# Two decode layers over a key-value cache: heads loaded in pairs with 64-KB runs into three slots, 21 cache parts kept between the layers, weights by column halves, layer norm applied to products

## The chip, the cores and the metric

The kernel runs on one core of a Trainium2 chip. The metric is the device time of one execution in microseconds (us), lower is better. All tensors are float32 in HBM when it begins, and the result must be in HBM when it ends. One core has five engines with queues of their own: PE (TensorE, matrix products), DVE (VectorE), ACT (ScalarE), POOL (GpSimd) and SP (SyncE, which here only issues transfers), and 16 DMA engines that share out each transfer by partitions. The on-chip memory has 128 partitions; 4-byte elements are counted as floats per partition below.

## The reference, cut to what matters

Two tokens (batch 2, one position) of width 576 pass the same layer twice: attention over a given cache of 32 heads, 8192 keys each, head width 128, then a gated MLP of width 4608. Both passes use the same weights and the same cache.

```python
B, H, Sk, Dh, D, DF = 2, 32, 8192, 128, 576, 4608
def attention(x):                 # x: [2, 1, 576]
    q = (x @ wq).reshape(B, 1, H, Dh).transpose(0, 2, 1, 3)
    scores = einsum("bhqd,bhkd->bhqk", q, k_cache) * Dh ** -0.5
    o = einsum("bhqk,bhkd->bhqd", softmax(scores), v_cache)
    return o.transpose(0, 2, 1, 3).reshape(B, 1, H * Dh) @ wo
def mlp(x):
    return einsum("bsf,fd->bsd", gelu_tanh(x @ w_gate) * (x @ w_up), w_down)
for layer in range(2):
    x = x + attention(layernorm(x))
    x = x + mlp(layernorm(x))
```

K and V of one head and batch are 4 MiB each; 64 such heads make 512 MiB, read in each layer. wq and wo are 9.4 MB each, gate, up and down 10.6 MB each.

## The kernel before, in words

**Memory.** One tile `space` holds six slots of 4 MiB (32 KB a partition; a partition holds 64 consecutive keys of a head) and 1024 floats more. All loads come from it and all are issued by SP, in the order of one list: `queue` is filled when the program is built, `pump()` (L117) issues its head as soon as its place is free, and `done()` (L124) frees a place and pumps. So a load is issued right after the instruction that frees its place, and everything behind it in the list waits with it. Which slot a head gets is settled by `Arena.slot`, the one that came free first.

**Attention, per head and batch** (64 items a layer; `attention`, the loop over `n`). `query` (L392) spreads the query over 128 partitions by a product on PE. K comes in one transfer (L134) and is used in four parts of 16 keys a partition (1 MiB): DVE multiplies a part by the query in place (`multiply`, L409), POOL adds the upper half of the 128 products to the lower (L413), and DVE sums what is left (`add_up`, L418), which frees the part. `peak` (L432, L434) and `highest` (L438, L440) find the maximum over all keys by DVE, a transposition on PE, and DVE again, and spread it. `softmax` (L444, L447) is two activations, `total` (L453, L457) the sum and its reciprocal. `values` (L469) is 16 groups of four products of 512 columns on PE, with four groups of columns filling the array side by side; each four groups free a part of V. `gather` (L483, L485) on DVE, `context` (L494) on PE and `divide` (L499) bring both batches of a head into place. The order on each engine is written out by hand in the loop: item n's multiplies stand between item n-1's softmax steps.

**The joints.** In layer 0 the heads run forward, in layer 1 backward, so the last heads of layer 0 stay for layer 1: K of two items and V of three, 20 parts of 1 MiB. For K that stays, the products go to a place of their own (`products`), since the multiply otherwise overwrites K. Weights of layer 0's MLP, of wo and of layer 1's wq run through one slot and 1024 floats, a ring of four pieces of 2304 floats; layer 1's MLP uses the whole space. First loads of layer 1 are taken part by part, in an order written out.

**Weights.** wq, gate and up come in nine pieces each (`eighths`, L165): a row is cut into eight, and a partition reads four neighbouring ones, 8 KB for wq, 9216 bytes for gate and up. `project` (L511) uses wo in eight pieces, `lower` down (L620) in pieces of three rows a partition (6912 bytes), the last cut into two and one. Products with two rows of x fill 128 columns by groups of four.

**Layer norm.** `norm` (L338 to L361) works out mean and deviation, subtracts the mean from x, transposes the result on DVE (L354), and the factor 1/deviation is applied by ACT when the products are read (L379, L591, L592). The first product of a stage waits for it.

Of the kernel before, what the change touches and what calls it, by code (L numbers as in the profile page):

```python
# [24 lines left out]
J = SK // P  # L25
NHB = H * B
JC = 16

GH = 4
NU = 9  # L30
EQ = 512
EG = DF // 8
HG = EG // 2
NT = 4
NI = DF // (NT * P)
CW = D // 4

SLOT = J * DH
PART = JC * DH
NSLOT = 6  # L40
END = NSLOT * SLOT + 1024
RING = 5 * SLOT
HELD = 5


class Arena:


    def __init__(self):
        self.live = {}  # L50
        self.freed = [0] * (NSLOT + 1)
        self.clock = 0
        self.at = RING

    def clear(self, lo, n):
        return all(hi <= lo or l >= lo + n for l, hi in self.live.values())

    def slot(self, key, allowed):

        for s in sorted(allowed, key=lambda s: self.freed[s]):  # L60
            if self.clear(s * SLOT, SLOT):
                for k in range(4):
                    self.quarter(key, s * SLOT, k)
                return s * SLOT
        return None

    def quarter(self, key, at, k):
        lo = at + k * PART
        if not self.clear(lo, PART):
            return False  # L70
        self.live[key, k] = (lo, lo + PART)
        return True

    def ring(self, key, n, lo, hi=None):

        for at in [self.at, lo] + sorted(end for _, end in self.live.values()):
            if lo <= at and at + n <= (hi or END) and self.clear(at, n):
                self.live[key] = (at, at + n)
                self.at = at + n
                return at  # L80
        return None

    def free(self, key):
        lo, hi = self.live.pop(key)
        self.clock += 1
        for s in range(lo // SLOT, (hi - 1) // SLOT + 1):
            self.freed[s] = self.clock
# [3 lines left out]
def decode_layers(ctx, tc, x_in, kc, vc, wq, wo, wg, wu, wd, out):  # L91
# [9 lines left out]

    space = consts.tile([P, END], F32, name="space")

    x = consts.tile([P, CW], F32, name="x")
    nc.vector.memset(x, 0.0)
    for c in range(4):
        for s in range(2):
            lo = 32 * c + s * B
            nc.scalar.dma_start(
                x[lo:lo + B, :], x_in[:, :, c * CW:(c + 1) * CW].rearrange("b s d -> (b s) d")  # L110
            )


    arena = Arena()
    queue, ready, slots = [], {}, {}

    def pump():  # L117
        while queue:
            t = queue[0][1]()
            if t is None:  # L120
                return
            ready[queue.pop(0)[0]] = t

    def done(key):  # L124
        arena.free(key)
        pump()

    def cache(key, src, hb, allowed, pieces=1, where=None, part=None):

        rows = src[hb % B, hb // B].rearrange("(p j) d -> p j d", p=P)  # L130

        def load(at, lo, hi):
            t = space[:, at:at + SLOT].rearrange("p (j d) -> p j d", d=DH)
            nc.sync.dma_start(t[:, lo:hi, :], rows[:, lo:hi, :])  # L134
            return t

        def make():
            at = arena.slot(key, allowed)
            if at is None:
                return None  # L140
            slots[key] = at
            for lo in range(0, J, J // pieces):
                t = load(at, lo, lo + J // pieces)
            return t

        def make_quarter(k):
            at = slots[key] = RING if where == "ring" else slots[where]
            return load(at, k * JC, (k + 1) * JC) if arena.quarter(key, at, k) else None

        if where is None:  # L150
            queue.append((key, make))
        else:

            for k in [(NU + i) % 4 if where == "ring" else i for i in range(4)] if part is None else [part]:
                queue.append((key, lambda k=k: make_quarter(k)))

    def eighths(key, w, u, width, lo, hi=None):

        def make():
            at = arena.ring(key, 4 * width, lo, hi)  # L160
            if at is None:
                return None
            t = space[:, at:at + 4 * width].rearrange("p (c w) -> p c w", c=4)
            src = w.rearrange("r (e w) -> (r e) w", w=width).rearrange("(p j) w -> p j w", p=P)
            nc.sync.dma_start(t, src[:, 4 * u:4 * u + 4, :])  # L165
            return t

        queue.append((key, make))

    def down(key, t0, lo, hi, first):  # L170

        def make():
            at = arena.ring(key, (hi - lo) * D, first)
            if at is None:
                return None
            t = space[:, at:at + (hi - lo) * D].rearrange("p (i c) -> p i c", c=D)
            src = wd[t0 * P * NI:(t0 + 1) * P * NI, :].rearrange("(p i) c -> p i c", i=NI)
            nc.sync.dma_start(t, src[:, lo:hi, :])
            return t

        queue.append((key, make))

    def products():

        def make():
            ends = [END - k * PART for k in (2, 1, 0)]
            if not arena.clear(ends[0], 2 * PART):
                return None
            for k in range(2):
                arena.live["products", k] = (ends[k], ends[k + 1])  # L190
            return ends[:2]

        queue.append(("products", make))

    def out_rows(key, g, lo):

        def make():
            at = arena.ring(key, GH * D, lo)
            if at is None:
                return None  # L200
            t = space[:, at:at + GH * D].rearrange("p (i c) -> p i c", c=D)
            rows = GH * DH
            nc.sync.dma_start(t, wo[g * rows:(g + 1) * rows, :].rearrange("(p i) c -> p i c", i=GH))
            return t

        queue.append((key, make))

    DOWN = [(t, lo, lo + 3) for t in range(NT) for lo in (0, 3, 6)]
    DOWN[-1:] = [(NT - 1, 6, NI - 1), (NT - 1, NI - 1, NI)]
    every, front = range(NSLOT), range(HELD)  # L210

    keys_held, values_held = range(NHB - 2, NHB), range(NHB - 3, NHB)

    weights_at = (RING, 0)

    def groups(layer):
        return range(H // GH)[::1 - 2 * layer]

    def plan_attention(layer, seq):
        for u in range(NU):  # L220
            if layer == 0:
                eighths(("wq", layer, u), wq, u, EQ, 3 * SLOT)
            else:

                at = RING + u % 4 * PART
                eighths(("wq", layer, u), wq, u, EQ, at, at + PART)

        def keys(n):
            hb = seq[n]
            held = hb in keys_held  # L230
            if layer == 1 and held:
                return


            where = {2: "ring", 3: ("k", 1, seq[0]), 5: ("v", 1, seq[1])}.get(n) if layer else None
            if layer and n == 4:
                for turn, k in (("k", 0), ("v", 0), ("v", 1), ("k", 1), ("v", 2), ("v", 3), ("k", 2), ("k", 3)):
                    if turn == "k":
                        cache(("k", 1, hb), kc, hb, None, where=("k", 1, seq[1]), part=k)
                    else:  # L240
                        cache(("v", 1, seq[3]), vc, seq[3], None, where=("v", 1, seq[0]), part=k)
                return

            allowed = every if layer or n < NHB - 3 else front
            cache(("k", 1 if held else layer, hb), kc, hb, allowed, where=where)

        def vals(n):
            hb = seq[n]
            held = hb in values_held
            if not (layer == 1 and (held or n == 3)):  # L250
                allowed = every if layer or n < NHB - 4 else front
                cache(("v", 1 if held else layer, hb), vc, hb, allowed, 4 if n == NHB - 1 else 1)

        for n in range(NHB + 1):
            if n < NHB - 1:
                keys(n)
            if n == NHB - 2:
                keys(n + 1)
            if n == NHB:

                if layer == 0:
                    products()
                for g in groups(layer)[:2]:
                    out_rows(("wo", layer, g), g, weights_at[layer])
            if n > 0:
                vals(n - 1)
        for g in groups(layer)[2:]:
            out_rows(("wo", layer, g), g, weights_at[layer])
# [394 lines left out]
```

## Time and profile before

| | us |
|---|---|
| median of three runs | 2715.41 (2715.26 to 2715.80) |
| span of the profiled execution | 2712.7 |
| DVE busy | 1887.1 (70%) |
| POOL busy | 1209.4 (45%) |
| PE busy | 1154.6 (43%) |
| mean DMA rate over the span | 426 GB/s |

The table is read from the page's head. The span is that of the profiled execution, from its first to its last instruction; the runs' time has 2.7 us more around it. Busy shares are averages: whether an engine or the DMA sets the pace has to be read from the slices and from the chain of waits. In the groups of instructions a row gives line, engine, operation, shapes, count, then busy time, the mean of one in ns, and the idle time ahead of them with what ended most of it. In rows of stretches, the columns are the stretch, its length, busy time (and count) of PE, PE's weight loads, DVE, ACT and POOL, then the granted PE clock, the DMA share (which can round to over 1) and GB/s. In rows of a schedule they are start, duration, engine, line, operation, and in brackets the idle time before it and its releaser.

### The profile page before, as it was taken

The page shows a single profiled execution, that of the slowest core. Times are in us where ns is not written, and L with a number is a line of the kernel's source. Part 1 is how long each engine was busy: PE and PEld are TensorE (multiplying, and loading weights), DVE is VectorE, ACT ScalarE, POOL GpSimd, SP SyncE. Part 2 cuts the span into 40 slices and gives each one's busy share as a digit, 9 for nine tenths or more (in the row PEclk, how much of TensorE's full clock was granted, in tenths as well). Part 3 has the DMA queues.
Part 4 walks back from the last instruction along what each step waited for, and adds up shares of the span by engine and source line. Part 5 has one row for each costly group of instructions (what it writes and reads, how often), then busy time and mean ns, then how long its engine had stood idle before and what let it go on. Part 6 is the DMA issues. An engine that isn't in the chain of part 4 may idle for free.

```text
span 2712.7 us, 19428 instructions
## 1 busy us (share of the span) xinstructions
PE 1154.6 (43%) x7392; PEld 404.2 (15%) x7392; DVE 1887.1 (70%) x1809; ACT 82.6 (3%) x391; POOL 1209.4 (45%) x522
## 2 busy tenths in 40 slices
PE   3343434343434333344645444343444343434355
PEld 0111111111111111111211111111111111111122
DVE  4777777777777777776039977777777777777740
ACT  0000000000000000000000000000000000000000
POOL 2444444444544454544016554545444444445420
PEclk7666666666666766666766756666656666566667
DMA  9999999999999999999999999999999999999998
GB/s 409 431 431 432 431 431 431 432 431 432 430 431 432 430 431 431 431 432 420 406 364 417 432 433 431 430 430 432 432 432 431 431 430 432 431 431 431 432 422 369
DMA packets 53132, 1155.49 MB, mean 426 GB/s; under 512 B 5912, under 2 KB 5936, under 8 KB 9264
## 3 DMA queue, kind: packets, MB, share of 16 engines
q1 hardware_dynamic: 53000, 1154.25, 99.5%
q8 instruction: 58, 0.95, 0.1%
q14 instruction: 34, 0.28, 0.0%
q10 hardware_dynamic: 40, 0.01, 0.0%
HBM read 1154.23 MB, written 0.00 MB: 425 GB/s over the span
## 4 chain that ended last, share of the span: by engine, by line
DMA 78%; DVE 11%; PE 8%; issue 2%; POOL 0%; SPq 0%; ACT 0%; ACTq 0%; DVEq 0%; POOLq 0%
DMA space<-in_A_k_cache_dram 46%; DMA space<-in_A_v_cache_dram 23%; PE acc L469 7%; DVE space L409 7%; DVE S L418 3%; DMA space<-in_A_wo_dram 3%; DMA space<-in_B_w_down_dram 2%; DMA space<-in_B_w_up_dram 2%; DMA space<-in_B_w_gate_dram 1%; DVE osb L485 1%; DMA space<-in_A_wq_dram 1%; POOL space L413 0%; PE acc L584 0%; PE xps L620 0%; DMA x<-in_A_x_dram 0%
## 5 line engine op out<-in xcount | busy, mean ns | idle before, releaser
L413 POOL TENSOR_TENSOR space<-space 128x1024 f32<-128x1024 f32 x512 | 1206.5, 2357 | 1265.1 <-DVE space L409 1226.8
L409 DVE TENSOR_TENSOR space<-space,qp 128x2048 f32<-128x2048 f32 x512 | 1164.6, 2275 | 486.5 <-DMA space<-in_A_k_cache_dram 464.6
L469 PE MATMUL acc<-space,prz 128*8 128x512 f32 x4096 | 733.6, 881 | 287.4 <-DVE osb L485 167.7
L418 DVE TENSOR_REDUCE S<-space 128x16 f32<-128x1024 f32 x512 | 615.9, 1203 | 3.3 <-POOL space L413 3.3
L434 PE MATMUL mT<-ident,m 128*1 128x128 f32 x128 | 46.9, 367 | 788.5 <-DVE m L432 788.5
L469 PEld LDWEIGHTS acc<-space,prz 128*8 128x8 f32 x4096 | 135.5, 116 | 772.4 <-issue 723.1
L440 PE MATMUL nb<-m,ones 1*128 1x1 f32 x256 | 74.1, 356 | 252.9 <-DVE m L438 252.9
L434 PEld LDWEIGHTS mT<-ident,m 128*1 128x1 f32 x128 | 10.1, 79 | 814.2 <-DVE m L432 808.3
L453 PE MATMUL tot<-rs,ones 128*128 128x1 f32 x256 | 74.7, 361 | 92.8 <-ACT prz L447 92.8
L440 PEld LDWEIGHTS nb<-m,ones 1*128 1x128 f32 x256 | 63.2, 305 | 289.7 <-DVE m L438 289.7
L444 ACT ACTIVATE nbs<-nb 128x1 f32<-128x1 f32 x128 | 21.9, 171 | 2363.2 <-PE nb L440 2363.2
L499 DVE TENSOR_TENSOR oT<-po,rinv 32x16 f32<-32x16 f32 x64 | 10.9, 170 | 115.7 <-PE po L494 115.7
L453 PEld LDWEIGHTS tot<-rs,ones 128*128 128x128 f32 x256 | 63.7, 309 | 104.0 <-ACT prz L447 103.5
L392 PE MATMUL qp<-qsb,pick 4*128 4x128 f32 x256 | 62.8, 327 | 32.0 <-DVE space L409 28.9
L360 POOL TENSOR_TENSOR rstd<-ve,mhalf 128x1 f32<-128x1 f32 x4 | 2.2, 552 | 164.6 <-DVE ve L358 164.6
L584 PE MATMUL acc<-space,xt 128*8 128x288 f32 x576 | 58.9, 548 | 38.9 <-DMA space<-in_B_w_up_dram 19.5
L485 DVE SCALAR_TENSOR_TENSOR osb<-acc,diag,osb 128x128 f32<-128x128 f32 x192 | 67.3, 351 | 6.8
L592 DVE TENSOR_SCALAR o<-acc,rstd 128x288 f32<-128x288 f32 x2 | 1.0, 517 | 95.7 <-ACT o L591 95.7
L392 PEld LDWEIGHTS qp<-qsb,pick 4*128 4x128 f32 x256 | 38.4, 188 | 92.5 <-PE acc L469 47.5
L364 DVE TENSOR_TENSOR x<-xps,x 128x144 f32<-128x144 f32 x4 | 1.2, 308 | 70.4 <-PE xps L620 40.8
L494 PEld LDWEIGHTS po<-of,osb 128*32 128x32 f32 x512 | 40.1, 151 | 49.6 <-issue 41.0
L447 ACT ACTIVATE prz<-S,nbs 128x64 f32<-128x64 f32 x128 | 44.5, 348 | 4.4 <-ACT nbs L444 0.4
(56 smaller groups left out, 328.7 us busy)
## 6 DMA issues: line engine op xcount, KB each, us to landing
space<-in_A_k_cache_dram SPq DMA_DIRECT2D x122, 4096.0 KB, 42.9
space<-in_A_v_cache_dram SPq DMA_DIRECT2D x122, 4096.0 KB, 45.1
space<-in_B_w_gate_dram SPq DMA_DIRECT2D x18, 1152.0 KB, 16.0
space<-in_B_w_up_dram SPq DMA_DIRECT2D x18, 1152.0 KB, 15.6
space<-in_B_w_down_dram SPq DMA_DIRECT2D x22, 864.0 KB, 11.0
space<-in_A_wq_dram SPq DMA_DIRECT2D x18, 1024.0 KB, 7.2
space<-in_A_wo_dram SPq DMA_DIRECT2D x16, 1152.0 KB, 20.8
space<-in_A_k_cache_dram SPq DMA_DIRECT2D x16, 1024.0 KB, 8.7
```

The source lines that it names most:

```text
L392: nc.tensor.matmul(qb[n], pick[32 * c:32 * c + 4, r:r + 1].to_broadcast([4, P]), qsb[32 * c:32 * c + 4, (h % 4) * DH:(h % 4 + 1) * DH], st ...
L409: nc.vector.tensor_tensor(out=u, in0=t, in1=qb[n].unsqueeze(1).to_broadcast([P, JC, DH]), op=ALU.mult)
L413: nc.gpsimd.tensor_tensor(out=half, in0=half, in1=u[:, :, DH // 2:], op=ALU.add)
L418: nc.vector.tensor_reduce(out=S[n][:, k * JC:(k + 1) * JC], in_=prod.pop((n, k)), axis=AX.X, op=ALU.add)
L434: nc.tensor.transpose(mT[n], m, ident)
L440: nc.tensor.matmul(mT[n], ones[0:1, :], m1, start=True, stop=True)
L447: nc.scalar.activation(pr, S.pop(n).rearrange("p (g r) -> p g r", r=4), AF.Exp, bias=nbs, scale=scale, accum_out=rs[n],)
L453: nc.tensor.matmul(tot, ones, rs.pop(n), start=True, stop=True)
L469: nc.tensor.matmul(acc[32 * c:32 * c + 8, (n // B) % 2, :], prz[:, n % 3, at:at + 8], t[:, 4 * g:4 * g + 4, :].rearrange("p j d -> p (j d) ...
L485: nc.vector.scalar_tensor_tensor(t, q[:, r, :], diag[:, r:r + 1], t, op0=ALU.mult, op1=ALU.add,)
L494: nc.tensor.matmul(po[lo:lo + 32, i, :], t[:, i::GH], of, start=True, stop=True)
L584: nc.tensor.matmul(acc[32 * c:32 * c + 4 * B, s, :HG], xt[:, 32 * u + at:32 * u + at + 4 * B], w[:, c, s * HG:(s + 1) * HG], start=(g == 0 ...
```

## The change

The kernel is written anew around a different block of the cache.

- **Pairs.** Heads 0 to 29 go in 30 pair items (two heads, one batch). A pair's K, and its V, is one transfer of 8 MiB: partitions 0 to 63 hold the first head, 64 to 127 the second, 128 consecutive keys each, 64 KB. Heads 30 and 31 remain four single items s0 to s3 of 4 MiB.
- **Three slots** of eight parts, and 768 floats more. K and V of pairs take turns through them in a fixed order, `slots0` in layer 0, `slots1` in layer 1.
- **Units.** A pair's K is multiplied in units of 2, 2, 2, 1 and 1 parts. `peak`, `highest`, `softmax`, `total` and `values` follow right after the last unit of their own item ("eager"), no longer among the next item's. `values` has 32 groups of four. The query tile `qp` is one tile with a place for even and one for odd items; `query(n + 1)` stands after the first unit of item n.
- **21 parts stay:** K of s3 and s2 and one part of s1, V of s3, s2 and s1. Products of K that stays go to `scratch` places, which are released when the sums of them are done; the places are later homes of V.
- **Weights by column halves.** A row of wq, gate or up is cut in two; a partition reads one half row (8 or 9 KB) or several neighbouring ones with 64-partition halves, and the middle rows come by themselves (`middle`, `middles`). Layer 0's wq is three transfers of 24, 24 and 16 KB a partition and the middle; layer 1's MLP has gate and up in pieces of 36 and 18 KB, down in pieces of 9, 9, 9, 5, 3 and 1 rows. In layer 1 the second half of wq comes first, and the first is used during item 0 (`rest_of_queries`). The ring in layer 0's MLP holds three pieces. The first half's gelu is done among the second half's products.
- **Layer norm on products.** x is transposed as it is (`turn`), and mean and deviation are folded into the small matrices `spread` and `chosen` that the products are next multiplied by, with a third row that carries the mean; `norm` comes after the first piece's products.

The order of loads, the core of the loop and the loads themselves in the changed kernel:

```python
def cache(kind, layer, item, at, lo=0, hi=None):
    hi = item.parts if hi is None else hi
    src = {"k": kc, "v": vc}[kind][item.b, item.h:item.h + item.heads].rearrange("h s d -> (h s) d")
    src = src.rearrange("(p j) d -> p (j d)", p=P)
    ...
        nc.sync.dma_start(space[:, a:a + (hi - lo) * PART], src[:, lo * PART:hi * PART])
...
slots0 = [P1, P2, P0]
slots1 = [P0, P2, P1]
for n, item in enumerate(pairs):
    for m, kind in enumerate("kv"):
        cache(kind, 0, item, slots0[(2 * n + m) % 3])
cache("k", 0, s0, P1)
cache("v", 0, s0, P1 + 4 * PART)
cache("k", 0, s1, home[("k",) + s1.name])
cache("k", 0, s2, home[("k",) + s2.name])
scratch(s1.name, P2, 1)
cache("v", 0, s1, home[("v",) + s1.name])
scratch(s2.name, P1 + 4 * PART)
cache("k", 0, s3, home[("k",) + s3.name])
cache("v", 0, s2, home[("v",) + s2.name])
scratch(s3.name, MID)
cache("v", 0, s3, home[("v",) + s3.name], 0, 2)
cache("v", 0, s3, home[("v",) + s3.name], 2, 4)
mid = sp.ring(MID, END)
for g in range(NG):
    out_rows(("wo", 0, g), mid, g)
...
for k in range(1, 4):
    cache("k", 1, s1, home[("k",) + s1.name], k, k + 1)
for k in range(4):
    cache("k", 1, s0, P1, k, k + 1)
for k in range(4):
    cache("v", 1, s0, P1 + 4 * PART, k, k + 1)
for n, item in enumerate(pairs[::-1]):
    for m, kind in enumerate("kv"):
        at = slots1[(2 * n + m) % 3]
        if n == m == 0:
            cache(kind, 1, item, at, 0, 4)
            cache(kind, 1, item, at, 4, 8)
        else:
            cache(kind, 1, item, at)
```

```python
query(0)
pending = None
for n in range(last + 1):
    item = items[n]
    eager = item.heads == 2 or n == last
    fresh = n > 0 and not (items[n - 1].heads == 2)
    for k, unit in enumerate(item.units):
        made = multiply(n, unit)
        if k == 0:
            if fresh:
                add_up(*pending)
                pending = None
                peak(n - 1)
            if n < last:
                if layer == 1 and n == 0:
                    query(1)
                    rest_of_queries()
                else:
                    query(n + 1)
        else:
            if k == 1 and fresh:
                highest(n - 1)
                softmax(n - 1)
                total(n - 1)
                values(n - 1)
            add_up(*pending)
            ...
            if k == 2 and n > 0:
                invert(n - 1)
        pending = made
        if k == len(item.units) - 2 and n > 0 and items[n - 1].heads == 2:
            gather(n - 1)
            context(n - 1)
        ...
    if eager:
        ...
        add_up(*pending)
        pending = None
        peak(n)
        highest(n)
        softmax(n)
        total(n)
        values(n)
```

And the core of the diff, where the cache and the slots are concerned:

```diff
-JC = 16
...
-SLOT = J * DH
-PART = JC * DH
-NSLOT = 6
-END = NSLOT * SLOT + 1024
+PART = 16 * DH
+P0, P1, P2 = 0, 8 * PART, 16 * PART
+END = 24 * PART + 768
+MID = 21 * PART
...
-    keys_held, values_held = range(NHB - 2, NHB), range(NHB - 3, NHB)
...
+    kept = {("k",) + s3.name: 4, ("k",) + s2.name: 4, ("k",) + s1.name: 1,
+            ("v",) + s3.name: 4, ("v",) + s2.name: 4, ("v",) + s1.name: 4}
+    home = {("v",) + s1.name: P2, ("k",) + s1.name: P2 + 4 * PART, ("k",) + s2.name: P0,
+            ("v",) + s2.name: P0 + 4 * PART, ("k",) + s3.name: P1, ("v",) + s3.name: P1 + 4 * PART}
...
-            qb[n] = psum2.tile([P, DH], F32, name="qp")
...
+    qp = psum1.tile([P, 2, 512], F32, name="qp")
```

More of the change, by code (lines that the diff above doesn't have):

```diff
@@ L58, in slot @@
[L58 to L78, printed above, removed]
-                self.at = at + n
-                return at
-        return None
+        self.queue = []
@@ L128, in cache @@
[L128 to L206, printed above, removed]
```

831 lines of the change are left out of this document (477 added, 354 removed).

## The prediction

> **What bounds the kernel now.** I read the page's head, its slices and its queue rows first, then the chain that ended last, then stretches of the run at the changes of stage.
>
> ```profile
> span 2712.7 us, 19428 instructions
> PE 1154.6 (43%) x7392; PEld 404.2 (15%) x7392; DVE 1887.1 (70%) x1809; ACT 82.6 (3%) x391; POOL 1209.4 (45%) x522
> DMA  9999999999999999999999999999999999999998
> GB/s 409 431 431 432 431 431 431 432 431 432 430 431 432 430 431 431 431 432 420 406 364 417 432 433 431 430 430 432 432 432 431 431 430 432 431 431 431 432 422 369
> DMA packets 53132, 1155.49 MB, mean 426 GB/s; under 512 B 5912, under 2 KB 5936, under 8 KB 9264
> q1 hardware_dynamic: 53000, 1154.25, 99.5%
> HBM read 1154.23 MB, written 0.00 MB: 425 GB/s over the span
> DMA 78%; DVE 11%; PE 8%; issue 2%; POOL 0%; SPq 0%; ACT 0%; ACTq 0%; DVEq 0%; POOLq 0%
> ...
> space<-in_A_k_cache_dram SPq DMA_DIRECT2D x122, 4096.0 KB, 42.9
> space<-in_A_v_cache_dram SPq DMA_DIRECT2D x122, 4096.0 KB, 45.1
> ```
>
> The DMA engines are busy in nearly every slice and the chain is 78% DMA. DVE, the busiest engine, has 30% to spare. In the attention slices 430 to 432 GB/s flow; 1154.23 MB at 431.5 would take 2675 us, so the span of 2712.7 holds some 38 us in which the transfers stand still or go slower. They are at the ends and in slices 19 to 22, where the stages change. The next view shows these stretches; the columns that matter are the last two, DMA share and GB/s.
>
> ```profile
> 100.00:600.00 500.00, 201.81 (x1106) 69.54 (x1098) 371.74 (x342) 15.31 (x75) 240.43 (x102) 0.64 1.00 431
> ...
> 1320.00:1330.00 10.00, 7.76 (x64) 1.74 (x64) 0.00 (x0) 0.00 (x0) 0.00 (x0) 0.52 1.01 419
> 1330.00:1340.00 10.00, 4.95 (x56) 1.23 (x56) 0.00 (x0) 0.00 (x0) 0.00 (x0) 0.82 1.01 423
> ...
> 1285.00:1295.00 10.00, 5.98 (x108) 3.26 (x104) 1.58 (x5) 0.00 (x0) 0.00 (x0) 0.68 0.88 345
> 1350.00:1370.00 20.00, 12.67 (x204) 7.44 (x208) 2.02 (x8) 0.76 (x2) 0.00 (x0) 0.59 0.82 306
> 1400.00:1430.00 30.00, 11.59 (x59) 3.67 (x59) 23.65 (x17) 1.30 (x4) 15.96 (x7) 0.58 0.87 337
> 2700.00:2712.70 12.70, 4.78 (x120) 2.59 (x120) 0.31 (x1) 0.00 (x0) 0.00 (x0) 0.97 0.37 149
> ```
>
> Idle DMA time: 0.12 x 10 = 1.2 us where the output projection's weights give way to the MLP's, 0.18 x 20 = 3.6 at the gelu, 0.13 x 30 = 3.9 where layer 1 begins: **about 9 us** at the changes of stage, and 8.0 in the last 12.7. So only three things can move the time: the bytes, what a packet costs beside its bytes, and time in which the queue on SP can issue nothing.
>
> **The change, part by part: what it takes off the transfers.**
> *Bytes.* 21 parts of 1 MiB stay in place instead of 20, so 1.05 MB less is read: at 431 GB/s **-2.4 us**.
> *Packets of the caches.* Before, 244 loads of 4 MiB are runs of 32 KB, one a partition: 128/16 = 8 packets an engine each, 1952. The 120 pair blocks are runs of 64 KB, 960 an engine, and the few 4-MiB loads at the joint stay. Some 960 packets an engine go. Their price: with 32-KB runs an engine carries 431/16 = 26.9 B/ns, so a packet takes 1216 ns; between 1320 and 1340 us, with 9216-byte runs, it carries 421/16 = 26.3, so a packet takes 350 ns. The line through both has 27.2 B/ns and 11.6 ns for the packet itself; with 423 alone, which is the better of the two rows, it has 9 ns. That stretch also holds pauses between narrow pieces, which push the estimate up, so I take 8 ns: 960 x 8 = **-7.7 us**, with 0 and -12 as ends.
>
> The Trainium skill (DMA: Bandwidth & Descriptors, section "Why small descriptors are slow (HBM only)") gives each packet about 3 cycles beside one for every 32 bytes. By that a 32-KB run would have 3 in 1027, and the saving would be about 4 us in place of 7.7. The rows above ask for two or three times that, and the sum does not use it.
>
> *Weights.* Layer 0's query weights go from nine runs a partition to four, layer 1's gate and up from 18 to seven, its downs from 13 to six: 23 x 8 = 184 packets an engine, **-1.5 us** by the same 8 ns. The middle rows and the MLP of layer 0 keep 9216-byte runs, and gain nothing.
> *Fewer transfers.* SP issues 217 loads instead of 366. The page counts 5912 packets under 512 B, 16 for each transfer, so each engine has one short packet less for each of the 149 that go: between 0 and 12 ns each, **-1 us** taken.
> Together **-12.6 us**.
>
> **What it adds: waits at the joints.** A pair load needs 8 parts free, the queue on SP is in order, and three slots are all there is. I follow the queue of the changed kernel, with DVE and PE times from the next rows: a stretch of the schedule in layer 1, then the groups.
>
> ```profile
> 1703.87 5.91 PE L469 MATMUL acc<-space,prz 128*8 128x512 f32 x32 [2.95 <-DVE osb L485]
> ...
> 1707.24 0.17 PEld L469 LDWEIGHTS acc<-space,prz 128*8 128x8 f32 x4 [0.69 <-issue]
> ...
> 1708.09 0.17 PEld L469 LDWEIGHTS acc<-space,prz 128*8 128x8 f32 x4 [0.69 <-issue]
> 1708.74 0.11 PEld L469 LDWEIGHTS acc<-space,prz 128*8 128x8 f32 x4 [0.48 <-issue]
> 1709.17 0.14 PEld L494 LDWEIGHTS po<-of,osb 128*32 128x32 f32 x1 [0.32 <-issue]
> ...
> 1712.34 2.29 DVE L409 TENSOR_TENSOR space<-space,qp 128x2048 f32<-128x2048 f32 x1 [1.95 <-DMA space<-in_A_k_cache_dram]
> 1714.54 1.21 DVE L418 TENSOR_REDUCE S<-space 128x16 f32<-128x1024 f32 x1
> ...
> 1715.78 0.33 SPq L134 DMA_DIRECT2D space<-in_A_v_cache_dram  x1
> ...
> 1715.92 2.28 DVE L409 TENSOR_TENSOR space<-space,qp 128x2048 f32<-128x2048 f32 x1
> ```
>
> ```profile
> L413 POOL TENSOR_TENSOR space<-space 128x1024 f32<-128x1024 f32 x512 | 1206.5, 2357 | 1265.1 <-DVE space L409 1226.8
> L469 PE MATMUL acc<-space,prz 128*8 128x512 f32 x4096 | 733.6, 881 | 287.4 <-DVE osb L485 167.7
> ```
>
> A multiply of one part and a reduce follow each other every 3.4 us on DVE. Values of one head take 5.9 us here, 733.6/128 = 5.7 on average.
>
> *End of layer 0.* V of single s1 has its home where s1's products of its one kept part lie (`scratch`), so its load waits for `add_up(s1, unit 0)`, and all later loads stand behind it. Count from the end of pair 29's last reduce. SP can then issue K s1; the load that ran ahead lasts some 6 us more (below), so K s1 and K s2, 4 MiB each at 431 GB/s = 9.7, keep the engines busy until 6 + 19.5 = 25.5. DVE meanwhile: s0's second multiply reads the query tile that `query(s1)` writes, and on PE this stands behind values(29): some 12.4 us (the loop below). Then three units of s0 at 3.4, s1's multiply, s0's last reduce and peak, and s1's second multiply and first reduce, some 18: the load is released at 30.4. From release to first bytes I take 1.5, an estimate: SP's issue is 0.33 in the row above, and what follows it no row gives alone; with 0.5 and 2.5 as ends it is 32. The engines stand for **6.5 us**.
> *First piece of `wo`* waits until s3's scratch is free, 2 to 3.5: **2.5**. *A ring of three* pieces instead of four in layer 0's MLP: a piece of 1.125 MiB lands in 1.18 MB/421 = 2.8 us; to hide, PE's use, the issue and the start must fit into 5.6 us, and they do except where products wait for norm or gelu: **1**, and for the query weights of layer 1, of which one half is used only during item 0, **3** (0 to 5).
> *Gelu:* its first half is done under the second half's weights, and one down piece runs ahead of the second: the 3.6 us of before go to about **0.5**.
> *Start of layer 1.* The second pair block needs slot P2, so it waits for values(s1), third in order. Transfers up to there: 4 of 1 MiB for the half of the query, 11 for K s1, K s0 and V s0, 8 for K of pair 29; three have landed when item 0 begins: 20 x 2.43 = 49 us. DVE and PE: three items of 4 x 3.4 = 41, from peak to total 3.4, values 5.9, waits for queries 3: 53 + 1.5. **5.8 us**, and 1 more for the block behind it.
> Together 6.5 + 2.5 + 4 + 0.5 + 6.8 = 20.3, where before had 9: **+11.3**, with ends 0 and +20. Start and tail have the same last pieces (288 KB down, one addition, the output): 0, give or take 1. The layer norm on products takes work off DVE only ahead of stages already counted.
>
> **Does the steady stream keep up?** A pair has 16.78 MB in two loads: 38.8 us at 432 GB/s. For DVE and PE there is a loop: second multiply of pair n (needs the query of n+1, which PE gives after values of n-1) to the last reduce, peak, softmax, values, query, second multiply of n+1. On DVE, by 2.2 us a part and 1.13 a part's reduce: multiplies of 2+2+1+1 parts 13.4, reduces of 8 parts 9.0, gather 1.4, wait for POOL's last half 0.2, reciprocal, the two maxima and their transposition 2: 26.0. Then the two small products 0.6 each, ACT about 1.1, and values of two heads in one go: the weight loads of the rows above come every 0.85 us at first and every 0.43 at the end, so 16 groups are 5 x 0.85 + 0.65 + 10 x 0.43 = 9.2 (8.5 to 11.4, the last being twice 5.7); query and the steps between engines 1: 38.5. It fits **by 0.3 us**. A K slot comes free about 4.5 + 26 + 2 = 32.5 us after its load has landed and is wanted after 38.8: the 6 us above.
>
> **The sum.** 2712.7 - 12.6 + 11.3 = 2711.4 of span. The median before is 2715.41, 2.7 above the profiled span, which I add: 2714.1. I give **2714**: within 0.2% (5.4 us), which is about what a measurement of this kernel can tell from no change.
>
> **The rivals.**
> 1. *Slower: the loop takes the place of the DMA.* If values of a pair take 10 us or each step between engines 0.1 more, the loop is 39.4. Past 38.8 + 6/30 = 39.0 the K slots come too late in the second half of each layer; at 39.4 the loss is (0.6 x 30 - 6) x 2 = 24, less what the joints then no longer cost (some 6): **2732**. For it: a margin of 0.3 from terms of 1% error. Against: the DVE durations are means of 512, and the multiply of 4096 elements saves one start in two. Chance 0.18.
> 2. *Faster: the joints cost as before.* SP's order and the release of single parts hide what I counted, 9 of 20 us, or the packets save 12: 2714 - 11 = **2703**. For it: the two largest joint terms are differences of two sums of 30 to 50 us. Chance 0.32.
> 3. *The change doesn't do what it says:* a 64-KB run is carried as two packets of 32 KB. Then 960 packets stay and the time is **2722**. The trace of before has no run over 32 KB. Chance 0.08.
> 4. *Longer strides are slower.* If rows 64 KB apart, 128 at a time, lose 1% of the rate against rows 32 KB apart, 2500 us of attention grow by 25: **2739**. No row of before excludes it; its 32-KB rows run at 431. Chance 0.08. The Trainium skill (DMA: Bandwidth & Descriptors, section "Latency and other measured facts") has copies losing speed where rows lie at large powers of two apart, from 512 KiB up, and none lost where tiles are laid out contiguously, as these are.
>
> **How the numbers follow.** The forecast, 2709 to 2720, has 0.34. Faster is rival 2, 0.32. Slower: rivals 1 and 4 and half of 3, 0.30. Same: the forecast and the other half of 3, 0.38. The range leaves out what of rival 2 is below 2702, and what of rivals 1 and 4 is above 2731: **2702 to 2731**. Its likeliest case alone reaches from 2709 to 2720.
>
> **What would show it.** Packets of q1 near 31,000, of which some 15,400 carry 64 KB; attention slices at 432 to 434 GB/s. If they stay at 431, the 8 ns are wrong; below 430, rival 4. In the waits of SP's queue, the longest at the end of layer 0 is behind s1's reduce, with a hole of 6 to 7 us in the DMA share, and one of 6 at the start of layer 1 behind PE's values; none over 1 us within the streams. If slices in the second half of a layer show idle DMA, with SP waiting for the K slot's last reduce, the loop is longer than 38.8 and rival 1 holds. At the gelu the hole of 3.6 should be gone.

## The result and the profile after

| | before | after |
|---|---|---|
| median, us | 2715.34 (2715.2 to 2715.8, 4 runs) | 2842.57 (2837.9 to 2844.73, 4 runs) |
| span of the profiled execution, us | 2712.7 | 2841.2 |
| DVE busy, us | 1887.1 | 2002.7 |
| MB read | 1154.23 | 1153.18 |

The changed kernel takes **1.0467 times** the time (95% interval 1.0452 to 1.0481): 127 us slower, where 2714 and a range of 2702 to 2731 were forecast. It is the first rival, the loop of DVE and PE in the place of the DMA, and much more of it than its price of 2732 said.

The page of the changed kernel, the lines that answer to those shown of before:

```profile
span 2841.2 us, 18902 instructions
PE 955.8 (34%) x7836; PEld 347.6 (12%) x7836; DVE 2002.7 (70%) x1330; ACT 93.1 (3%) x419; POOL 1173.6 (41%) x342
GB/s 428 427 428 402 427 400 413 410 416 401 413 415 409 404 412 416 412 392 311 379 350 380 440 414 416 416 412 400 427 400 413 400 428 400 414 399 427 399 417 389
q1 hardware_dynamic: 30744, 1153.19, 95.9%
DVE 26%; PE 14%; DMA 7%; issue 5%; POOL 2%; ACT 1%; POOLq 0%; SPq 0%; DVEq 0%
...
L480 DVE TENSOR_TENSOR space<-space,qp 128x4096 f32<-128x4096 f32 (+1 forms) x332 | 1140.9, 3437 | 511.3 <-PE qp L452 413.7
L490 DVE TENSOR_REDUCE S<-space 128x32 f32<-128x2048 f32 (+1 forms) x332 | 594.4, 1790 | 85.7 <-POOL space L484 85.7
L551 PE MATMUL acc<-space,prz 128*8 128x512 f32 x4096 | 595.9, 746 | 0.0
...
L543 DVE TENSOR_TENSOR weights<-of,rinv 128x2 f32<-128x2 f32 (+1 forms) x68 | 149.5, 2199 | 2.4
```

The row of the kernel before that answers to L480:

```profile
L409 DVE TENSOR_TENSOR space<-space,qp 128x2048 f32<-128x2048 f32 x512 | 1164.6, 2275 | 486.5 <-DMA space<-in_A_k_cache_dram 464.6
```

Three readings. The chain was 78% DMA; now DVE has 26% of it, PE 14% and DMA 7%. DVE's multiply waited for K before (464.6 of 486.5 us); it now waits for the query (413.7 of 511.3 us). And L543, a product of two elements a partition, lasts 2.2 us on average, as long as a multiply of 2048: DVE's busy time is 116 us longer than before though it has fewer instructions.

One turn of a pair, in order of time. The rows to see are the second multiply (621.33), the reciprocal and the product behind it (634.39, 634.58), and the addition on POOL that began at 632.44:

```profile
607.79 0.33 SPq L136 DMA_DIRECT2D space<-in_A_v_cache_dram  x1
...
610.32 4.42 DVE L480 TENSOR_TENSOR space<-space,qp 128x4096 f32<-128x4096 f32 x1 [1.49 <-DMA space<-in_A_k_cache_dram]
...
611.70 9.22 PE L551 MATMUL acc<-space,prz 128*8 128x512 f32 x64
...
621.33 4.42 DVE L480 TENSOR_TENSOR space<-space,qp 128x4096 f32<-128x4096 f32 x1 [6.58 <-PE qp L452]
...
632.44 4.50 POOL L484 TENSOR_TENSOR space<-space 128x2048 f32<-128x2048 f32 x1 [2.03 <-DVE space L480]
634.39 0.16 DVE L541 RECIPROCAL rinv<-tot 128x2 f32<-128x2 f32 x1
634.58 2.38 DVE L543 TENSOR_TENSOR weights<-of,rinv 128x2 f32<-128x2 f32 x1
636.88 2.28 DVE L480 TENSOR_TENSOR space<-space,qp 128x2048 f32<-128x2048 f32 x1
...
647.51 1.22 DVE L490 TENSOR_REDUCE S<-space 128x16 f32<-128x1024 f32 x1 [1.41 <-POOL space L484]
...
662.29 4.42 DVE L480 TENSOR_TENSOR space<-space,qp 128x4096 f32<-128x4096 f32 x1 [6.48 <-PE qp L452]
```

The product ends at 636.96, and POOL's addition at 636.94. The next V load is issued at 648.76, 40.97 us after that of 607.79, so a pair takes 41.0 us instead of the 38.8 that its bytes need.

The same stretches of both kernels, in the order before, after; a stretch ends where x has been added to. The length less its bytes at 431.5 GB/s is the time lost in it.

```profile
100.00:1200.00 1100.00, 443.94 (x2442) 154.29 (x2434) 819.89 (x760) 34.30 (x168) 530.37 (x225) 0.64 1.00 431
1200.00:1302.00 102.00, 49.36 (x469) 20.29 (x469) 61.77 (x64) 3.06 (x15) 37.69 (x16) 0.67 0.99 418
1302.00:1381.00 79.00, 48.63 (x614) 17.99 (x614) 4.38 (x17) 0.76 (x2) 0.56 (x1) 0.70 0.96 387
1381.00:1480.00 99.00, 47.31 (x244) 13.00 (x244) 73.35 (x65) 3.14 (x13) 47.64 (x21) 0.66 0.97 399
1480.00:2580.00 1100.00, 455.83 (x2460) 157.69 (x2460) 838.50 (x779) 35.50 (x174) 541.53 (x230) 0.63 1.00 431
2580.00:2712.70 132.70, 75.99 (x993) 31.26 (x992) 29.30 (x47) 1.99 (x8) 15.07 (x8) 0.74 0.95 395
```

```profile
100.00:1200.00 1100.00, 333.66 (x2457) 116.10 (x2457) 827.32 (x486) 35.36 (x162) 488.91 (x135) 0.63 0.97 412
1200.00:1372.90 172.90, 71.07 (x650) 29.05 (x650) 119.78 (x105) 7.58 (x37) 68.88 (x25) 0.65 0.86 358
1372.90:1456.20 83.30, 54.56 (x650) 20.36 (x650) 6.37 (x32) 1.29 (x4) 0.70 (x1) 0.65 0.97 371
1456.20:1560.00 103.80, 50.96 (x286) 15.38 (x286) 86.93 (x85) 5.25 (x24) 51.89 (x20) 0.69 0.91 369
1560.00:2700.00 1140.00, 345.80 (x2540) 120.14 (x2540) 857.19 (x501) 36.67 (x168) 506.41 (x139) 0.62 0.97 413
```

| lost, us | before | after |
|---|---|---|
| the two streams | 1.3 + 1.3 | 49.7 + 48.9 |
| end of layer 0 | 3.2 | 29.5 |
| MLP of layer 0 | 8.1 | 11.7 |
| start of layer 1 | 7.5 | 15.0 |

Some 96 of the 128 us are lost evenly in the streams and the rest at the joints.

### The profile page after: what moved, and what is told of

The parts are those of the page before. It is cut to its first block, busy times and chain, and to the rows that moved or that the text cites. A ratio compares the mean times of both kernels' runs of the same rounds, so it can differ in the third digit from the quotient of the medians.

```text
span 2841.2 us, 18902 instructions
## 1 busy us (share of the span) xinstructions
PE 955.8 (34%) x7836; PEld 347.6 (12%) x7836; DVE 2002.7 (70%) x1330; ACT 93.1 (3%) x419; POOL 1173.6 (41%) x342
## 3 DMA queue, kind: packets, MB, share of 16 engines
q1 hardware_dynamic: 30744, 1153.19, 95.9%
HBM read 1153.18 MB, written 0.00 MB: 406 GB/s over the span
## 4 chain that ended last, share of the span: by engine, by line
DVE 26%; PE 14%; DMA 7%; issue 5%; POOL 2%; ACT 1%; POOLq 0%; SPq 0%; DVEq 0%
DVE space L480 11%; PE acc L551 10%; DVE S L490 9%; DVE weights L543 3%; DMA space<-in_B_w_down_dram 3%; POOL space L484 2%; DMA space<-in_B_w_gate_dram 2%; DVE osb L563 1%; DMA space<-in_A_k_cache_dram 1%; PE nb L511 1%; ACT prz L523 1%; DMA space<-in_A_wo_dram 1%; PE tot L533 1%; DMA space<-in_B_w_up_dram 1%; PE qp L452 0%
## 5 line engine op out<-in xcount | busy, mean ns | idle before, releaser
L484 POOL TENSOR_TENSOR space<-space 128x2048 f32<-128x2048 f32 (+1 forms) x332 | 1170.1, 3525 | 1439.7 <-DVE space L480 1397.3
L480 DVE TENSOR_TENSOR space<-space,qp 128x4096 f32<-128x4096 f32 (+1 forms) x332 | 1140.9, 3437 | 511.3 <-PE qp L452 413.7
L490 DVE TENSOR_REDUCE S<-space 128x32 f32<-128x2048 f32 (+1 forms) x332 | 594.4, 1790 | 85.7 <-POOL space L484 85.7
L551 PE MATMUL acc<-space,prz 128*8 128x512 f32 x4096 | 595.9, 746 | 0.0
L571 PE MATMUL po<-weights,osb 128*32 128x1 f32 x1024 | 59.5, 201 | 1260.3 <-DVE osb L563 1260.3
L571 PEld LDWEIGHTS po<-weights,osb 128*32 128x32 f32 x1024 | 54.1, 154 | 1278.3 <-DVE osb L563 1278.1
L543 DVE TENSOR_TENSOR weights<-of,rinv 128x2 f32<-128x2 f32 (+1 forms) x68 | 149.5, 2199 | 2.4
L511 PE MATMUL nb<-m,strip 1*128 1x1 f32 x256 | 64.5, 350 | 38.8 <-DVE m L508 38.8
L511 PEld LDWEIGHTS nb<-m,strip 1*128 1x128 f32 x256 | 58.7, 313 | 57.6 <-DVE m L508 54.6
L523 ACT ACTIVATE prz<-S,nbs 64x128 f32<-64x128 f32 (+1 forms) x136 | 53.4, 393 | 3.1
L662 PE MATMUL acc<-space,xt 128*6 128x288 f32 x256 | 28.9, 588 | 26.3 <-DMA space<-in_B_w_up_dram 15.4
```

Of the source, the lines that this page charges most:

```text
L480: nc.vector.tensor_tensor(out=u, in0=t, in1=qp[:, n % 2, 0:DH].unsqueeze(1).to_broadcast([P, j, DH]), op=ALU.mult)
L484: nc.gpsimd.tensor_tensor(out=half, in0=half, in1=u[:, :, DH // 2:], op=ALU.add)
L490: nc.vector.tensor_reduce(out=S[n][:, 16 * lo:16 * hi], in_=half, axis=AX.X, op=ALU.add)
L511: nc.tensor.matmul(low[n], one_of[e] if heads == 2 else ones[0:1, :], m1[:, e:e + 1], start=(e == 0), stop=(e == heads - 1),)
L523: nc.scalar.activation(prz[rows_, n % 2, 0:item.rows // 4, e, :], s[rows_, 0:item.rows].rearrange("p (g r) -> p g r", r=4), AF.Exp, bias=n ...
L543: nc.vector.tensor_mul(weights[n], of[:, 0:2] if heads == 2 else of[:, 2:3], rinv)
```

## The experiments

"On-chip memory" stands here for SBUF, where `space` and most small tiles lie; PSUM is the other memory on the chip, which takes PE's products. Theory A: the product that makes the weights (L543) waits until POOL's addition has ended, its 2.38 us lie in the loop of DVE and PE, and this loop, 41.0 us, has taken the place of the DMA. Rivals: the transfers of 64-KB runs are slow themselves (B), or the small product has that price wherever it stands (C).

**One operand in PSUM (e1_psum).**

```diff
-            rinv = work.tile([P, heads], F32, name="rinv")
-            nc.vector.reciprocal(rinv, low.pop(n))
+            rinv = low.pop(n)
+            nc.vector.reciprocal(rinv, rinv)
```

> One edit: the reciprocal is written back into its PSUM place, so that the 128x2 product that makes the weights has one operand in PSUM instead of two in on-chip memory. Theory A (the product waits for POOL's addition, 2.38 us in the loop of DVE and PE, and the loop is the bound): the product takes 0.16 to 0.2 us, a pair's period falls from 40.96 to about 38.75 us, just the 38.7 that 8 MiB twice need, and the time falls to 2712 to 2722 us. Theory B (64-KB runs or the slots make the transfers slow, and DVE and PE wait for them): the period stays near 41 and the time within 10 us of 2842. Theory C (the small product is dear wherever its operands lie): it stays at 2.2 to 2.4 us, the time near 2842.

Measured: 2725.11 us, 1.0032 of before (1.0018 to 1.0045). The product takes 156 ns (durations as min, median, max):

```profile
L543 DVE TENSOR_TENSOR weights<-of,tot x68: 155/156/158, 103.3 to 2638.1; 128x2 f32<-128x2 f32 x60, 128x1 f32<-128x1 f32 x8
```

DVE's waits between 100 and 1200 us have changed sides. First the changed kernel, then this one (columns: us in total, times, longest):

```profile
DVE space L480 <- PE qp L452: 184.4, 27, 7.8
DVE S L490 <- POOL space L484: 38.1, 27, 1.4
DVE space L480 <- DMA space<-in_A_k_cache_dram: 32.9, 27, 5.3
```

```profile
DVE space L480 <- DMA space<-in_A_k_cache_dram: 198.2, 28, 8.7
DVE S L490 <- POOL space L484: 39.8, 28, 1.7
DVE space L480 <- PE qp L452: 27.4, 28, 2.0
```

DVE waits 7.1 us a pair for K again, and 1.0 for the query. One operand's place was worth 117 us. The time is 3 us above the range given, and that is not in the streams, which run at 432 GB/s, 38.9 us a pair. It is at the joints, the end of layer 0 above all:

```profile
1200.00:1309.60 109.60, 58.13 (x543) 24.05 (x543) 66.22 (x74) 6.11 (x30) 39.97 (x17) 0.67 0.87 359
```

18.4 us are lost there, against 3.2 before. A loop of some 38.6 us under a DMA of 38.8 gains no lead.

**The product moved (e2_moved).**

```diff
+                    if n > 0 and not fresh:
+                        invert(n - 1)
...
-                    if k == 2 and n > 0:
+                    if k == 2 and n > 0 and fresh:
```

> One edit: reciprocal and product of a pair stand behind the first multiply of the next pair, where DVE then waits 6.6 us for the query, instead of behind the third. Operands unchanged. Theory A: the product may still last up to 4.6 us (an addition of 2048 elements on POOL starts at the same moment), but under the wait for the query, so the period is again about 38.75 and the time that of the run with the PSUM operand, within 5 us. If it is not the place in the loop that matters but DVE's busy sum, the time falls by no more than a few us from 2842.

Measured: 2728.94 us, 1.0052 (1.0037 to 1.0067), 3.8 above the run before it, as expected. The product was not hidden under a wait, though: it got ahead of POOL, which starts behind it.

```profile
632.40 0.16 DVE L541 RECIPROCAL rinv<-tot 128x2 f32<-128x2 f32 x1
632.59 0.16 DVE L543 TENSOR_TENSOR weights<-of,rinv 128x2 f32<-128x2 f32 x1
632.71 4.52 POOL L484 TENSOR_TENSOR space<-space 128x2048 f32<-128x2048 f32 x1 [13.79 <-DVE rinv L541]
```

The same instruction with the same operands takes 0.16 us here (the median) and 2.38 there: who comes first decides.

**Two query tiles (e3_two_qp).**

```diff
-    qp = psum1.tile([P, 2, 512], F32, name="qp")
+    qp = [psum1.tile([P, 512], F32, name="qp%d" % i) for i in range(2)]
```

> One edit: the query tile is two tiles of one bank each, so that the second multiply no longer waits for the next item's query, which stands behind values on PE. The product stays as it is, 2.38 us. Theory A (the loop is closed by this wait): without it DVE has some 33 us of work a pair, under the DMA's 38.7, and the time falls to 2703 to 2716 us, although the 2.38 us are still there. Theory B: near 2842. If only the product mattered and not the loop: near 2842 too.

Measured: 2721.73 us, 1.0021 (1.0011 to 1.0031). With the 2.38 us still on DVE (busy 2003.6 us), 121 us are gone, so it was the loop that made them dear. Item n's multiply reads only item n's half of the query tile; as one tile it waited for the write of the other half too, and with two tiles no wait for the query is left among DVE's waits between 100 and 1200 us. The streams run at 432 and 433 GB/s, so the 5.7 us above the range are at the joints.

**The product twice (e4_twice).** The second product's result is the same as the first's.

```diff
             nc.vector.tensor_mul(weights[n], of[:, 0:2] if heads == 2 else of[:, 2:3], rinv)
+            if heads == 2:
+                nc.vector.tensor_mul(weights[n], of[:, 0:2], rinv)
```

> The product of a pair is made twice in a row, the second time in vain. Lock theory (it waits until POOL's addition has ended): the second finds POOL idle, takes 0.16 us, and the time grows by about 60 x 0.2 = 12 us, to 2855. Theory C (2.2 us is the operation's own price): the second takes as long, and 60 x 2.4 = 140 us come on top, 2985.

Measured, one run: 2848.98 us, 6 below what the lock theory gave. First the one product, then the other:

```profile
L543 DVE TENSOR_TENSOR weights<-of,rinv x68: 159/2380/2385, 103.2 to 2760.7; 128x2 f32<-128x2 f32 x60, 128x1 f32<-128x1 f32 x8
```

```profile
L545 DVE TENSOR_TENSOR weights<-of,rinv x60: 160/161/163, 105.6 to 2760.9; 128x2 f32<-128x2 f32 x60
```

Theory C falls: the operation's own price is 0.16 us.

**A spare product in the kernel before (b_lock, b_lock_late).** In the first it stands behind the reciprocal:

```diff
             nc.vector.reciprocal(rinv[n // B][:, b:b + 1], tot)
+            spare = work.tile([P, 1], F32, name="spare")
+            nc.vector.tensor_mul(spare, rinv[n // B][:, b:b + 1], ones[:, 0:1])
```

> The kernel before, with one product of 128x1 by 128x1, both in on-chip memory, added after each reciprocal, in vain. Lock theory: it starts while POOL adds the halves of the third part, 2.36 us, and ends with it: 1.5 to 2.4 us each, 128 x 2 = 250 us more on DVE (70% to about 79%). Since DVE is not in a loop with the DMA there, that is covered: 2714 to 2722 us. Rival (any small product is 0.16 us here): DVE's busy time grows by 20 us only.

Measured: 2716.91 us, 1.0005 (0.9996 to 1.0014), but DVE grew by 29 us only. The expectation missed: the product comes some 0.05 us before POOL's start there, and goes first; three of the 128 last 2.3 us, the others 0.16. So it was put later:

```diff
             add_up(n, 1)
+            if before:
+                spare = work.tile([P, 1], F32, name="spare")
+                nc.vector.tensor_mul(spare, diag[:, 0:1], ones[:, 0:1])
             multiply(n, 3)
```

> The kernel before with a spare product of 128x1 by 128x1, both in on-chip memory, this time behind the reduce of the second part, when POOL has been adding the third part's halves for some 1.2 of its 2.36 us. Lock theory: it lasts until POOL ends, 1.0 to 1.3 us each time, 126 times, so 125 to 165 us more on DVE, and the time stays within 4 us of the kernel before, since DVE has cover there. Rival (a small product takes 0.16 us unless it is issued at POOL's very start): 20 us more on DVE.

Measured: 2716.45 us, 1.0004 (0.9995 to 1.0014).

```profile
L553 DVE TENSOR_TENSOR spare<-diag,ones x126: 148/1380/1420, 58.8 to 2599.1; 128x1 f32<-128x1 f32 x126
```

DVE's busy time grew by 93 us, less than the 125 to 165 expected. The median hides two kinds, which take turns: 66 of the 126 products last more than 1 us and 59 last 0.15. Two neighbours, with the addition on POOL ahead of each:

```profile
114.35 2.35 POOL L413 TENSOR_TENSOR space<-space 128x1024 f32<-128x1024 f32 x1 [1.16 <-DVE space L409]
115.33 1.38 DVE L553 TENSOR_TENSOR spare<-diag,ones 128x1 f32<-128x1 f32 x1
...
133.79 2.35 POOL L413 TENSOR_TENSOR space<-space 128x1024 f32<-128x1024 f32 x1 [1.17 <-DVE space L409]
136.17 0.15 DVE L553 TENSOR_TENSOR spare<-diag,ones 128x1 f32<-128x1 f32 x1
```

The first starts while POOL adds, and ends at 116.71, POOL at 116.70. The second comes at 136.17, when POOL has ended at 136.14. So the wait for POOL is there in the kernel before as well, up to 1.42 us wherever POOL is at work, and it costs nothing, since DVE has cover.

**Both edits (f_both).** The diffs of e1_psum and e3_two_qp together.

> Both edits of the first runs together: two query tiles, and the product with one operand in PSUM. Loop theory: with two query tiles alone DVE already had 33 us of work for a pair that the DMA needs 38.7 for, so taking 2.2 us more off DVE can give nothing in the streams; at the end of layer 0 DVE runs a little ahead. 2715 to 2722 us, against 2721.7 with the two tiles alone. If DVE's work still set the pace anywhere in the streams, the time would fall by up to 60 x 2.2 = 130 us, far below.

Measured: 2714.61 us, 0.9999 (0.9989 to 1.0009), a little under the range. The streams are the DMA's again, and the 7 us less than with two tiles alone come at the joints; which DVE instruction there does it wasn't separated.

**Runs of 32 KB (f32_runs).** f_both, with each pair block in two transfers:

```diff
-                cache(kind, 1, item, at)
+                cache(kind, 1, item, at, 0, 4)
+                cache(kind, 1, item, at, 4, 8)
...
-            cache(kind, 0, item, slots0[(2 * n + m) % 3])
+            cache(kind, 0, item, slots0[(2 * n + m) % 3], 0, 4)
+            cache(kind, 0, item, slots0[(2 * n + m) % 3], 4, 8)
```

> The kernel with both edits, each pair block loaded as two transfers of 4 MiB, so with runs of 32 KB instead of 64 KB; slots, order and releases as before. Packet theory (8 to 10.5 ns for each packet beside its bytes, some 950 an engine, and one more short packet for each of 119 transfers): slower by 8 to 11 us than the kernel with both edits in the same call. Rival (the length of a run has no price, the better rate in the streams came from elsewhere): within 3 us of it.

Measured: 2719.82 us, 1.0018 (1.0009 to 1.0027): 5.2 us slower than f_both, less than expected. The streams, f_both first:

```profile
100.00:1200.00 1100.00, 345.45 (x2564) 120.75 (x2564) 815.98 (x516) 36.80 (x169) 517.91 (x143) 0.61 1.00 432
...
1485.00:2585.00 1100.00, 343.33 (x2561) 121.03 (x2561) 810.47 (x514) 36.80 (x169) 512.63 (x142) 0.61 1.00 433
```

```profile
100.00:1200.00 1100.00, 349.52 (x2565) 121.58 (x2562) 808.45 (x509) 37.53 (x173) 512.13 (x141) 0.61 1.00 431
1490.00:2590.00 1100.00, 354.20 (x2619) 123.46 (x2623) 810.32 (x513) 37.96 (x174) 512.28 (x141) 0.61 1.00 431
```

1 and 2 GB/s in 431.5 over 1100 us each are 7.6 us, but rounding leaves 3 to 13. The time from one pair's maximum to that of the 25th after it says it more exactly: 970.8 us in f_both and 974.8 here, in both layers, so 0.157 us a pair and 9.4 for the sixty, as expected. That is 8.7 ns for each of the 18 packets an engine that a pair has more (16 of the data, and one short one for each of two transfers more); the two kinds weren't separated. The half blocks give some 4 us of it back outside the streams, perhaps by an earlier first multiply, which wasn't tried by itself. Theory B falls: the longer runs are the faster ones.

**20 parts and a ring of four (f20_ring4).** f_both, without the 21st part and its scratch place; 1024 floats in place of 768, for which the norm's small tiles have one buffer instead of two.

```diff
-END = 24 * PART + 768
-MID = 21 * PART
+END = 24 * PART + 1024
+MID = 20 * PART
...
-    kept = {("k",) + s3.name: 4, ("k",) + s2.name: 4, ("k",) + s1.name: 1,
+    kept = {("k",) + s3.name: 4, ("k",) + s2.name: 4, ("k",) + s1.name: 0,
...
-    scratch(s1.name, P2, 1)
...
-    for k in range(1, 4):
+    for k in range(4):
```

> The kernel with both edits, but with 20 parts kept (none of K s1, so no scratch place that V s1 waits for) and a ring of 4 parts and 1024 floats, which is four pieces of 2304 floats instead of three. Theory on the rest of the loss (it sits at the joints: three pieces starve the DMA in layer 0's MLP, and V s1 waits for its scratch place): layer 0's MLP, from one addition to x to the next, falls from 85 to 78 to 80 us, the end of layer 0 loses 3 to 6 us less, one part more is read, 2.4 us: 2706 to 2714. Rival (short packets or the middle rows make that stage slow): the stage stays at 85 and the time within 4 us of the kernel with both edits.

Measured: **2698.98 us, 0.9939 (0.9924 to 0.9953)**, the fastest version, 17 us under the kernel before and 7 below the range expected. Its ring cut to three tells which half did it:

```diff
-    mid = sp.ring(MID, END)
+    mid = sp.ring(MID, MID + 3 * HF)
```

> The fastest kernel so far (both edits, 20 parts kept, ring of four pieces) with its ring cut to three pieces of 2304 floats; nothing else changed, 21st part still not kept. If the ring is what made layer 0's MLP slow: that stage, from one addition to x to the next, goes from 75.8 back to about 83 us and the time from 2699.0 to 2704 to 2709. If the place that the 21st part takes away mattered otherwise (scratch place of s1, order at the joint): the stage stays near 76 and the time within 3 us of 2699.

Measured: 2710.74 us, 0.9985 (0.9976 to 0.9995), 11.8 above the ring of four and 2 above the range expected. The MLP of layer 0, ring of four first:

```profile
1296.70:1372.50 75.80, 51.06 (x650) 19.89 (x650) 6.32 (x31) 1.29 (x4) 0.70 (x1) 0.70 1.01 420
```

```profile
1299.80:1383.60 83.80, 56.48 (x650) 20.93 (x650) 6.38 (x32) 1.29 (x4) 0.70 (x1) 0.60 0.96 369
```

Eight of the 11.8 us are in this stage, lost by three pieces in flight instead of four, and 3.1 ahead of it, where wo passes the same ring. Without the 21st part but with the ring of three, the time is 3.9 us under f_both, though 1 MB more is read.

## Why the prediction was wrong, by its own steps

*The loop (the step that failed).* Its sum was 38.5 us, "fits by 0.3 us". In it, the reciprocal stood with the maxima and the transposition for 2 us, and the product behind it, `weights`, had no term at all; it was passed over as one more small operation. It lasts 2.38 us, since both its operands lie in on-chip memory while POOL adds. The rest of the sum came out: from the second multiply (621.33) to the next one (662.29) is 40.96 us, less 2.38 is 38.6. Term by term it came out partly by luck. The wait for POOL's last half was given 0.2 us and took 1.4 (the row at 647.51): behind one part's multiply POOL adds for 2.35 us, and DVE has only a reduce of 1.2 to fill that time. The reciprocal, maxima and transposition took 1.3 instead of 2, and multiplies and reduces 22.1 instead of 22.4, so the two errors nearly cancel. The nearest row of before could not show the product's price: no product there has both operands in on-chip memory during a POOL addition (L409 and L499 read PSUM), and b_lock_late shows that one would have waited.

The Trainium skill (SBUF — State Buffer, section "Who interferes with whom") states it: a DVE instruction with two inputs in SBUF contends with a GpSimd instruction that reads SBUF, and whichever starts first holds the shared ports for its whole length. The runs agree: 2.38 us behind POOL's start, 0.16 ahead of it, 0.156 with one input in PSUM.

*Rival 1's price.* The mechanism and the point from which it decides, 39.0, were right; the chance of 0.18 rested on terms of 1% error, and not on a missing term of 6%. At 41.0 its own formula gives (2.2 x 30 - 6) x 2 = 120, less 6, so 2828. The streams lost 96 more than before, so what makes up 2842 is at the joints as far as the stretches tell, which a loop without lead makes longer, not shorter: 26.3 us more at the end of layer 0 (of which the loop took some 3, since 63 us of the stream lie in the stretch), 3.6 in its MLP and 7.5 at the start of layer 1, where 7.8, -2.1 and 5.9 were forecast.

*End of layer 0.* The hole was put at 6.5 us, with a lead of 6 by the load that ran ahead. In the changed kernel there is no lead left, and the hole is 0.88 x 15 = 13.2 us, where 6.5 + 6 = 12.5 would be expected (no run shows by itself the 1.5 us from release to first bytes that is part of the 6.5):

```profile
1285.00:1300.00 15.00, 4.32 (x35) 2.81 (x39) 13.76 (x13) 1.20 (x6) 7.05 (x3) 0.50 0.12 33
```

With the loop off the path (f_both) the stretch has a share of 0.95 and 392 GB/s over 100.9 us, 9.2 lost against 3.2 before: 6.0 more, where 6.5 + 2.5 - 1.2 = 7.8 was forecast.

*The ring of three* was mis-sized: 1 us was given it, and 3.1 us of gain by the earlier gelu. f20_ring3 against f20_ring4 measured 8.0 in the MLP alone. The gain is there with four pieces: the stage takes 75.8 us against 79.0 before, and around its last gelu, from 1340 to 1370 us, the DMA share is 1.00 to 1.02 in each 10 us, so the hole of 3.6 us is gone. How much of the gain is the gelu's and how much the later layer norm's wasn't separated. Why 5.6 us of other pieces don't cover a start of 1.5 (the prediction's estimate), products of 2.1 and an issue of 0.33 isn't settled: the share stays at 0.96 while the rate falls to 369 GB/s, so the loss shows as packets that take longer and hardly as idle engines.

*Start of layer 1:* 5.8 + 1 + 3 - 3.9 = 5.9 more was forecast, 7.5 came (15.0 against 7.5), and 3.4 in f_both.

*Bytes and packets* were right: 1.05 MB less, 30744 packets, 8 ns a packet foreseen and 8.7 measured (f32_runs against f_both). The streams' 9.4 us are more than twice the 4 that the prediction worked out by the Trainium skill's 3 cycles a packet (DMA: Bandwidth & Descriptors, section "Why small descriptors are slow (HBM only)"). Rivals 3 and 4 fell with it: 30744 packets leave no room for split runs, and the streams of f_both run at 432 and 433 GB/s. The 1.5 us for the weights and the 1 for fewer transfers weren't tested by themselves.

*What is left without the failed step.* The fair test is e1_psum, where only the product's wait is gone: 2725.1, 11 us above the forecast. There the streams are as forecast, and the joints dearer: 15.2 us more than before at the end of layer 0, where 7.8 were forecast, and 5.9 more in the MLP, where 2.1 less were. That f_both at 2714.61 stands at the forecast of 2714 is in part luck: its second query tile, which takes the loop off the path, is no part of the change, and the ring was dearer and the start of layer 1 cheaper than summed.

## What to carry to other kernels

Where a loop over several engines fits by less than its smallest term, list each instruction in it by line, with operands, before calling it covered; an instruction's price in a loop is its wait, not its size. On DVE beside a busy POOL, give small products of two tensors one operand in PSUM, or issue them ahead of POOL. And a part more kept in memory is dear if it takes a piece from a ring: 1 MB less to read is worth 2.4 us at 431 GB/s, and the ring of three cost 11.8 against the ring of four.

## What the runs showed of the hardware that was not expected

A product of 128x2 elements with both operands in SBUF lasts 2.38 us when POOL's addition of 2048 elements is under way, and ends with it; ahead of POOL it lasts 0.16. In the trace that wait is no idle time: it is part of the product's recorded duration. The reductions, and the multiplies with one operand in PSUM, ran beside the same additions at their usual durations (2.28 us; 4.41 beside an addition, 4.42 without). In the MLP of layer 0 a DMA share of 0.96 stands beside 369 GB/s (f20_ring3) and beside 387 (the kernel before): the share is no rate.
